# Changing the priority of the pole parameters, the patience for host stages and the order of the turned matmuls in a fused S4D and MLP kernel

## The chip, the core and the metric

The kernel runs on one NeuronCore of a Trainium2 chip. The metric is the device time of one launch in microseconds (us). The engines are TensorE (PE, the matmuls; its weight loads are listed as PEld), VectorE (DVE), ScalarE (ACT), GpSimd (POOL) and SyncE (SP, which here only issues DMAs). Each engine takes its instructions in program order and waits for others by semaphores. All matmuls write to PSUM, which has eight banks here called `cv` (four, as two pairs), `m0` to `m3`.

## The reference

```python
x  = A_u                                   # 1 x 2048 x 576
xn = layernorm(x)
# S4D: a long convolution along the 2048 positions, per channel d
A = -exp(log_A_real) + 1j * A_imag;  C = (C_real + 1j * C_imag) * dt      # 576 x 128, dt = exp(log_dt)
K[d, l] = 2 * Re(sum_n C[d, n] * exp(A[d, n] * dt[d] * l))
s = causal_convolution(xn, K) + xn * D_skip     # by an FFT of length 4096
# channel MLP on the same xn, with a second layernorm
h = gelu(layernorm(xn) @ w1 + b1)          # 2048 x 4608
g = silu(h @ w2 + b2)                      # 2048 x 576
out = x + s * g
```

Everything is float32. The kernel multiplies with the type fp32r and splits each operand of the MLP in a high and a low part, so that every product becomes three matmuls (high times high, high times low, low times high).

## The kernel before, in words

**The MLP carries the time axis.** The 4608 hidden units are cut into 12 groups of 384 (`NG = 12`, `G = 3` blocks of 128). The 2048 tokens are cut into two halves, and each half into two blocks of 512 tokens (`tb`). One group of one token block is a slot; there are 48 slots, in the order of `SETS`. A slot has 11 positions. The first three are layer 1, one block of 128 hidden units each: 14 matmuls of 512 columns (L546) into one bank, then gelu and a copy on ACT (L578, L581: `h`, `hh`) and a subtraction on DVE (L584: `hl`). The other eight are layer 2, in the order of the list `PLAN`, each entry a key and the hidden blocks it takes. The output's 576 columns are cut in 448 plain and 128 turned ones. A plain key 0 to 3 is a block of 128 tokens: stationary `hh` or `hl`, moving `w2s` with 448 columns (L638), into a bank that DVE then adds to `acc` (L643). The key `"T"` is the turned part: stationary `w2s`, moving `hh` or `hl` with 512 tokens (L630), accumulated in a bank of its own over many slots. Two banks, `m0` and `m1`, serve layer 1 and the plain keys by turns. Four slots (`TURNED`) use another form with 288 columns (L608, added by L615).

**Weights.** Each weight set (a group's `w1` and `w2`) comes through the tile `raw` by DMAs on SP (L473 to L478) and is split by ACT (L530) and DVE (L527) while the previous matmuls run. A set in `JOINED` has its `w2` split in three rows of 576 columns; any other is split apart, in 448, 384 and 896 columns, with the turned part as the second. `NEXT` says how many further raw loads each split issues: 1, 2, 2 for a joined `w2`, and 1, 0, 4 for one apart.

**The S4D part rides on the MLP.** Its matmuls are put between the positions of the slots. First come the parameters: `params()` builds from the four tables of poles and coefficients a polar form (magnitude, frequency and phase per pole), in the line `pl`: log_A_real is turned (L800) and goes through exp (L802), then C_real and C_imag are turned (L800), squared, and so on to an arctangent and sines (ACT) with reciprocals (DVE), then A_imag is turned. The four tables are fetched on SP (L793) at planned times in the list `fetch`. The result is packed and stored (`par_s`). Then 36 table stages make sines and magnitudes, and 36 guests (`kgen`, L981, 64 small matmuls each) turn them into the convolution's kernel. Six chunks of 96 channels each go through the stages `k1`, `x1` (L1053), `s2` (L1092), `inv` (L1145) and `i1` (L1177); these are the hosts. `i1` is followed by the stores of `s_s` (L1188). At the end, `combine_load`, `gated` (L711) and `summed` (L716) put together the output of the first half of the tokens, and `last_s` (L732), `finish` (L751 to L770) that of the second half.

**A planner sets the order.** The kernel is unrolled, and the order of all instructions on each engine is made by the class `Order`: it keeps an estimated clock for each engine, and lines of steps, each with an estimated length, a due time and the marks it needs. `advance` takes the step that can start first; of several that can start at the same time, the one whose line stands first in `od.lines`. In the early slots `row_lines` (L1333 on) rearranges that list. The line `nl` holds the layer norms of the blocks 4 to 15 of the tokens (L383 to L405); before the change it stands right ahead of `pl`. The order that comes out is fixed; if an engine is later in truth than in the plan, what stands behind waits.

**Where hosts and guests go.** `pe_turns` is called after every position, and on the positions given in `all_lines` it may put a host or a guest on PE. A paced host (`k1`, `x1`, `s2`) must come at least half of `(END - now) / left` after the one before it, `left` being the paced hosts still to come. A guest that is ready when a host is placed goes ahead of it in the same place (`ride`). Once the hosts have begun, a guest that finds no host goes alone when it has been ready for `ALONE` us (the last guest is exempt).

Of the kernel before, what the change touches and what calls it, by code (L numbers as in the profile page):

```python
# [23 lines left out]
NCH = D // CH  # L24
# [11 lines left out]
G = 3  # L36
# [7 lines left out]
def dve(n):  # L44
    return 0.075 + 0.00104 * n
# [163 lines left out]
def step(eng, dur, fn, need=(), mark=None, cv=0, at=0.0, late=0.0, tbl=None, by=1e9):  # L209
    return dict(eng=eng, dur=dur, fn=fn, need=tuple(need), mark=mark, cv=cv, at=at, late=late, tbl=tbl, by=by)  # L210
# [3 lines left out]
def mixer_kernel(ctx, tc, u, log_a_real, a_imag, c_real, c_imag, log_dt, d_skip, w1, b1, w2, b2,  # L214
# [238 lines left out]
    SEQ = [(n, g, tb) for n, (g, tbs) in enumerate(SETS) for tb in tbs]  # L453
    FIRST, GATE = (0, 3, 2 * NG, 2 * NG + 1), (2 * NG - 4, 2 * NG - 1)
    TURNED = (2 * NG - 4, 2 * NG - 1, 4 * NG - 2, 4 * NG - 1)
    JOINED = {SEQ[slot][0] for slot in TURNED} | set(range(6))
    DT = D - DA
    for n, (g, _) in enumerate(SETS):
        PARTS += [(n, g, 1, i) for i in range(KB + 1)] + [(n, g, 2, i) for i in range(G)]
# [37 lines left out]
    def split_raw(low_on=nc.vector):  # L497
# [14 lines left out]
        else:  # L512
            joined, m = half in JOINED, P
            if i == 0:
# [178 lines left out]
    def combine_load(b, n, c0, c1, part=None):  # L693
        m = c1 - c0
        if part is None:
            XS[b] = [sb.tile([P, D], F32, name="row", bufs=NROW)[:, :n * m].rearrange("p (i d) -> p i d", i=n) for _ in range(3)]
        elif part == 0:
            kt = [sb.tile([P, 12, 64], F32, name="kt", bufs=2).rearrange("p a b -> p (a b)") for _ in range(2)]
            xc = sb.tile([P, 2, 32, 24], F32, name="xc", bufs=NXC).rearrange("p a b c -> p (a b c)")
            XS[b] = [t[:, :n * m].rearrange("p (i d) -> p i d", i=n) for t in (kt[0], xc, kt[1])]  # L700
        x, s, g = XS[b]
        if part != 1:
            nc.gpsimd.dma_start(x, u_s[:, b:b + n, c0:c1])
            nc.gpsimd.dma_start(g, g_s[b:b + n, :, c0:c1].rearrange("i p d -> p i d"))
        if part != 0:
            nc.gpsimd.dma_start(s, s_s[:, b:b + n, c0:c1])
# [71 lines left out]
    def params():  # L778
# [10 lines left out]
        T = [p[:, :D] for p in PRM] + [ys_tile().rearrange("p i a b c -> p (i a b c)")[:, :D]]  # L789

        def load(k):
            for q in range(4):
                nc.sync.dma_start(PRM[k][32 * q:32 * q + 32, :D].rearrange("p (b j) -> p b j", j=32), dram(  # L793
                    src[k], 32 * q, [[N, 32], [32 * N, D // 32], [1, 32]]))
        fetch = [step(None, 6.0, lambda k=k: load(k), at=t, mark=("praw", k)) for k, t in ((0, 44.0), (2, 56.0), (3, 60.0), (1, 66.0))]
        add(None, 12.0, lambda: nc.sync.dma_start(dt, dram(log_dt, 0, [[0, P], [1, D]])), at=24.0)
        add("ACT", act(D), lambda: nc.scalar.activation(dt, dt, AF.Exp), tbl="exp", late=0.0)
        V, A = nc.vector, nc.scalar
# [16 lines left out]
        t = T[2]  # L815
# [394 lines left out]
    NPOS = G + 8  # L1210
    NSLOT = 4 * NG
    od = Order(tc, nc)
    od.pinned = True
    el, wl2, wl, nl2, pl, pl2, pl3, pl4, pl5, nl, ml, ml2, xl, wx, c3, c2, c1, kl, tl, sl, vl, gl, fl, f2l = [od.line() for _ in range(24)]
# [78 lines left out]
    MA, MT = 0.2034, 0.2303  # L1293
    CONV = {2 * NG - 6: 0, 2 * NG - 2: 1, 4 * NG - 4: 0, 4 * NG - 3: 1}
    both, allof = (0, 1), (0, 1, 2)
    PLAN = [("T", both), (0, both), ("T", (2,)), (0, (2,)), (1, allof), (2, allof), (3, (0,)), (3, (1, 2))]
    ENDS = {True: {2: 0, 3: 1, 5: 2, 7: 3}, False: {3: 0, 4: 1, 5: 2, 7: 3}}

    def lens(slot):
# [32 lines left out]
    def row_lines():  # L1332

        Y = [A2F[:, k:k + TB] for k in (2 * D, PT0 + 4 * D, 0, D, PT0 + 4 * D + TB, PT0 + 4 * D + 2 * TB)]
        X, T = [Y[k] for k in (0, 1, 2, 0, 3)], Y[4:]

        def store(t):
            nc.gpsimd.dma_start(dram(y4_s, t * P * D, [[D, 64], [64 * D, 2], [1, D]]), YT[4 + t])

        def load(i):  # L1340
            for q in range(4 if i < KB else 2):
                y = X[i][32 * q:32 * q + 32]
                if i < KB:
                    nc.gpsimd.dma_start(y.rearrange("p (b d) -> p b d", b=4), dram(
                        y4_s, i * P * D + P * q, [[D, 32], [32 * D, 4], [1, P]]))
                else:
                    nc.gpsimd.dma_start(y.rearrange("p (b j) -> p b j", j=32), dram(
                        y4_s, KB * P + 32 * q, [[D, 32], [32 * D, NT], [1, 32]]))

        def blocks(i):  # L1350
            x, y = T[i % 2], X[i]
            if i < KB:
                nc.vector.transpose(x.rearrange("p (k b t) -> p k b t", k=4, b=4),
                                    y.rearrange("p (b k j) -> p k b j", k=4, b=4))
            else:
                nc.vector.transpose(x[:64], y[:64])

        def places(i):
            y = T[i % 2]
            c = slice(i * P, (i + 1) * P)  # L1360
            if i < KB:
                return y.rearrange("p (k t) -> p k t", k=4), XH[:, :, 1, c], XL[:, :, 1, c]
            return y[:64], XR[:64, 1], XR[64:, 1]

        def high(i):
            y, h, _ = places(i)
            nc.scalar.activation(h, y, AF.Copy)

        def low(i):
            y, h, lo = places(i)  # L1370
            nc.vector.tensor_sub(lo, y, h.bitcast(F32))
        issue = od.line()
        for i in range(KB + 1):
            out = od.line()["steps"]
            if i < KB:
                out.append(step("POOL", 0.7, lambda i=i: store(i), need=[("yn", 4 + i)], mark=("yo", i)))
            out.append(step(None, 6.0, lambda: None, need=[("yo", min(i, 3))], mark=("ys", i)))
            issue["steps"].append(step("POOL", 2.4 if i < KB else 1.2, lambda i=i: load(i), mark=("yi", i),
                                       need=[("ys", i)] + ([("yt", 0)] if i == 3 else [])))
            od.line()["steps"].append(step(None, 5.0 if i < KB else 7.0, lambda: None, need=[("yi", i)], mark=("yl", i)))  # L1380
            a, b, c = od.line(), od.line(), od.line()
            a["steps"].append(step("DVE", dve(TB), lambda i=i: blocks(i), mark=("yt", i),
                                   need=[("yl", i)] + ([("y2", i - 2)] if i > 1 else [])))
            b["steps"].append(step("ACT", act(TB), lambda i=i: high(i), mark=("yh", i), need=[("yt", i)]))
            c["steps"].append(step("DVE", dve(TB), lambda i=i: low(i), need=[("yh", i)], mark=("y2", i) if i < KB else ("x", 1)))
        k = [i for i, x in enumerate(od.lines) if x is pl][0]
        od.lines = od.lines[-26:] + od.lines[:k] + [nl] + [x for x in od.lines[k:-26] if x is not nl]

    YB = []

# [102 lines left out]
    for k in range(4):  # L1493
        gl["steps"].append(step("POOL", 5.0, lambda k=k: part.update({k: load_g2(k)}), mark=("g2", k),
                                need=[("g2c", k - 1)] if k else []))
# [24 lines left out]
    def end_line():  # L1520
        for c, c0, c1, sets in ((NCH - 3, 0, CE, [(b, 1) for b in range(8)]), (NCH - 2, CE, CL, [(0, 4), (4, 4)])):
            for b, n in sets:
                a = (b, n, c0, c1)
                ml["steps"].append(step(None, 8.0 if b else 12.0, lambda a=a: combine_load(*a), need=[("st", c), ("u", NT - 1)]))
                ml["steps"].append(step("DVE", 2 * dve(n * (c1 - c0)), lambda a=a: (gated(*a), summed(*a))))
                ml["steps"].append(step(None, 4.0, lambda: None))
        a = (0, 8, CL, D)
        ml["steps"].append(step(None, 1.0, lambda: combine_load(*a, 0), need=[("k1", NCH - 1, 1), ("x1", NCH - 1)]))
        ml["steps"].append(step(None, 11.0, lambda: combine_load(*a, 1), need=[("st", NCH - 1)]))
        ml["steps"].append(step("DVE", dve(8 * CH) + 0.1, lambda: gated(*a)))  # L1530
        ml["steps"].append(step("DVE", dve(8 * CH) + 0.1, lambda: summed(*a)))


    pace = dict(left=NCH * (2 + 2 + 4), last=0.0, started=False)
    END = 930.0
    ALONE = 5.0

    def pe_turns(limit=1, any_time=False, all_lines=True):
        for x in (nl, pl, ml) + ((c3, c1, kl) if all_lines else ()):
# [29 lines left out]
    later(mid - 4, G - 1, lambda: x_free(0))  # L1569
    later(mid - 1, G - 1, lambda: x_free(1))  # L1570
    later(NSLOT - 10, 4, end_line)
    sl["steps"].append(step(None, 11.0, last_s, need=[("st", NCH - 1)], mark="s8"))
    for k in range(8):
        c3["steps"].append(step(None, 5.0 if k == 0 else 2.0, lambda k=k: last_x(k), need=[("i1", NCH - 1), ("u", NT - 1)], mark=("x8", k)))

# [49 lines left out]
    for slot in range(NSLOT):  # L1625
# [4 lines left out]
        for pos in range(NPOS):  # L1630
            if pos < G:
                need = wmark(n, 1) + [("x", tb)]
# [16 lines left out]
                for k, (a, b, c) in enumerate(cell, pos + 1 - len(cell)):  # L1649
                    by = hidden_by(pos, k)  # L1650
                    if slot == NSLOT - 1 and k:
                        a = seeded(a, tb, k)
# [6 lines left out]
            else:  # L1659
# [6 lines left out]
                need = [wmark(n, 2)[i] for i in w2_parts(n, j, hid)] + [("h", slot, i) for i in hid]  # L1666
# [19 lines left out]
                if last or halves:  # L1686
                    add = cell[0]
                    dh, k = (terms[0][1], 1) if halves else (0, 2)
# [9 lines left out]
                    if final:  # L1698
                        b = 8 + 4 * tb + j
                        x, y = (el, el2) if slot < NSLOT - 1 else (od.line(),) * 2  # L1700
# [13 lines left out]
            for f in LATER.get((slot, pos), ()):  # L1714
                f()
            od.advance(od.t["PE"])
            pe_turns(all_lines=pos in (0, 1, G + 1, G + 3, G + 5, NPOS - 1))
    od.force(lambda: not od.urgent and not any(x["steps"] for x in od.lines))


# [52 lines left out]
```

## Time and profile before

| what | value |
|---|---|
| median of 3 runs | 1068.91 us (1068.3 to 1071.31) |
| the profiled execution | 1070.33 us |
| its span, first to last instruction | 1068.2 us |
| PE busy | 1057.6 us, 99% |
| DVE busy | 936.7 us, 88% |
| ACT busy | 677.4 us, 63% |
| POOL busy | 212.2 us, 20% |
| granted PE clock | 0.999 |

The profile is of one execution. Its time differs from the span by what lies before the first and after the last instruction. A row of the order of time gives the start, the length, the engine and line, what is written and read, the shapes, how many instructions are merged in the row, and in brackets the engine's idle time before it with what ended it. Matmuls are pipelined: the length of one is longer than the step from its start to the next one's start, and it is the step that adds up. A row of a stretch gives its bounds and length, then for PE, PEld, DVE, ACT and POOL the busy time and the count, then the PE clock, the DMA share and GB/s.

### The profile page before, as it was taken

How to read it: one execution, taken by the hardware profiler on the slowest of the kernel's cores; microseconds unless marked ns; L12 is line 12 of the kernel's file. 1: busy time of each engine (PE TensorE's matmuls, PEld its weight loads, DVE VectorE, ACT ScalarE, POOL GpSimd, SP SyncE). 2: the span in 40 equal slices, each digit the busy share in tenths (PEclk: the TensorE clock that was granted, in tenths of full speed). 3: DMA queues.
4: the chain of work that ended last, by engine and by line, in shares of the span. 5: the costliest groups of instructions: out<-in, count | busy, mean ns of one | idle time of the engine just before them, and what ended most of it. 6: DMA issues, size and time to landing. Idle time of an engine off the chain costs nothing. (4 is left out here: it accounts for less than half of the span.)

```text
span 1068.2 us, 23535 instructions
## 1 busy us (share of the span) xinstructions
PE 1057.6 (99%) x9515; PEld 874.5 (82%) x9515; DVE 936.7 (88%) x1550; ACT 677.4 (63%) x1056; POOL 212.2 (20%) x294
## 2 busy tenths in 40 slices
PE   9999999999999999999999999999999999999997
PEld 7887888888878887888878888788877888778886
DVE  7688768889999899999999999899899999957656
ACT  6567639877655767657667675666685675625344
POOL 5668743201000002000120000200002022322020
PEclk9999999999999999999999999999999999999999
DMA  7885446664223143454521315222421446465145
GB/s 230 238 259 171 121 144 224 214 163 142 62 69 91 43 100 99 120 134 116 124 83 48 110 39 121 74 75 64 96 86 45 132 118 150 125 188 162 24 126 170
DMA packets 149213, 130.93 MB, mean 123 GB/s; under 512 B 99020, under 2 KB 121072, under 8 KB 148080
## 3 DMA queue, kind: packets, MB, share of 16 engines
q1 hardware_dynamic: 132592, 79.76, 28.2%
q0 software_dynamic: 15760, 48.70, 14.9%
q8 instruction: 75, 1.23, 0.5%
q10 hardware_dynamic: 752, 0.97, 0.3%
q14 instruction: 34, 0.28, 0.1%
HBM read 98.90 MB, written 35.19 MB: 126 GB/s over the span
## 5 line engine op out<-in xcount | busy, mean ns | idle before, releaser
L638 PE MATMUL m<-w2s,hh 128*128 128x448 f32 x1056 | 301.9, 367 | 0.4 <-DVE acc L643 0.2
L638 PEld LDWEIGHTS m<-w2s,hh 128*128 128x128 f32 x1056 | 196.1, 188 | 28.9 <-issue 7.0
L578 ACT ACTIVATE h<-m,b1t 128x512 f32<-128x512 f32 x144 | 99.2, 689 | 188.2 <-PE m L546 183.6
L638 PE MATMUL m<-w2s,hl 128*128 128x448 f32 x528 | 191.5, 363 | 0.0
L546 PE MATMUL m<-XH,w1h 128*128 128x512 f32 x564 | 155.5, 398 | 0.0
L546 PE MATMUL m<-XL,w1h 128*128 128x512 f32 x564 | 151.6, 391 | 0.0
L546 PE MATMUL m<-XH,w1l 128*128 128x512 f32 x564 | 151.0, 390 | 0.0
L584 DVE TENSOR_TENSOR hl<-h,hh 128x512 fp32r<-128x512 f32 x144 | 99.1, 689 | 53.7 <-ACT hh L581 53.3
L546 PEld LDWEIGHTS m<-XH,w1h 128*128 128x128 f32 x564 | 103.4, 188 | 30.9 <-issue 9.1
L546 PEld LDWEIGHTS m<-XL,w1h 128*128 128x128 f32 x564 | 105.9, 188 | 23.0
L546 PEld LDWEIGHTS m<-XH,w1l 128*128 128x128 f32 x564 | 105.9, 188 | 22.4
L881 POOL DMA_DIRECT2D par<-par_s x36 | 27.4, 762 | 484.2 <-DVE mg L924 423.7
L643 DVE TENSOR_TENSOR acc<-m,acc 128x448 f32<-128x448 f32 x160 | 98.4, 615 | 19.0 <-PE m L638 17.7
L638 PEld LDWEIGHTS m<-w2s,hl 128*128 128x128 f32 x528 | 99.1, 188 | 7.4
L630 PE MATMUL m<-hh,w2s 128*128 128x512 f32 x264 | 98.9, 402 | 0.0
L581 ACT ACTIVATE hh<-h 128x512 fp32r<-128x512 f32 x144 | 90.6, 630 | 3.3
L530 ACT ACTIVATE w2s<-raw 128x576 fp32r<-128x576 f32 (+3 forms) x75 | 46.4, 675 | 48.6 <-PE m L638 47.0
L924 DVE TENSOR_TENSOR mg<-par 128x1024 f32<-128x1024 f32 x72 | 67.9, 952 | 0.7
L630 PEld LDWEIGHTS m<-hh,w2s 128*128 128x128 f32 x264 | 49.6, 188 | 17.5 <-issue 5.1
L527 DVE TENSOR_TENSOR w1l<-raw,w1h 128x384 fp32r<-128x384 f32 x98 | 49.8, 558 | 13.8 <-ACT w1h L530 13.7
L546 PE MATMUL m<-XR,w1r 128*128 128x512 f32 x141 | 54.9, 389 | 0.0
L546 PE MATMUL m<-XR,w1s 128*128 128x512 f32 x141 | 54.9, 389 | 0.0
(227 smaller groups left out, 1866.3 us busy)
## 6 DMA issues: line engine op xcount, KB each, us to landing
raw<-in_B_w_dram SPq DMA_DIRECT2D x75, 288.0 KB, 3.5
raw<-in_B_w_dram SPq DMA_DIRECT2D x100, 192.0 KB, 3.4
par_s<-A POOLq DMA_DIRECT2D x8, 1080.0 KB, 5.6
par<-par_s POOLq DMA_DIRECT2D x36, 240.0 KB, 3.4
f2t<-f2q SPq DMA_DIRECT2D x24, 256.0 KB, 3.8
raw<-in_B_w_dram SPq DMA_DIRECT2D x50, 96.0 KB, 3.9
u_s<-in_A_u_dram POOLq DMA_DIRECT2D x16, 288.0 KB, 4.1
xc<-xn_s SPq DMA_DIRECT2D x48, 96.0 KB, 4.1
```

What stands on the lines that cost most here:

```text
L527: low_on.tensor_sub(lo, r[:m], h[:m].bitcast(F32))
L530: nc.scalar.activation(h, r, AF.Copy)
L546: nc.tensor.matmul(q, a, b, start=j == 0, stop=j == len(ops) - 1)
L578: nc.scalar.activation(t, q, AF.Gelu_apprx_tanh, bias=b1t[:, g * G + i:g * G + i + 1], scale=1.0)
L581: LAST[0] = nc.scalar.activation(hh[:, i], t, AF.Copy)
L584: nc.vector.tensor_sub(hl[:, i], t, hh[:, i].bitcast(F32))
L630: nc.tensor.matmul(q, a[:, i], b[:, i], start=first and i == 0 and k == 0, stop=slot in CONV and i == G - 1 and k == 2, skip_group_check=True)
L638: nc.tensor.matmul(q[:, :DA], a[:, i, key * P:key * P + P], b[:, i], start=i == 0 and k == 0, stop=i == G - 1 and k == 2)
L643: nc.vector.tensor_add(o, Q2.pop(key)[:, :DA], bias2[:, :DA] if first else o)
L881: nc.gpsimd.dma_start(PAR[b].rearrange("p (g i) k -> p g (i k)", g=4), dram(par_s, (b // 6 * CH + b % 6 * 4) * NPAR, [[D * NPAR, P], [24 * ...
L924: nc.vector.tensor_mul(T["m"][:, :, 64 * k:64 * k + 8 * n].rearrange("p c (i j) -> p c i j", i=n), bc(PAR[b][:, :, e8:e8 + n], 3, 8), bc(P ...
```

## The change

Seven edits are made together.

- `JOINED` keeps only the weight sets 0 and 1 of the first six; the sets 2 to 5 are now split apart.
- The list `fetch` asks for C_real first, at 44, then log_A_real at 50, C_imag at 56 and A_imag at 62. Before, it was log_A_real at 44, C_real at 56, C_imag at 60 and A_imag at 66.
- `PLAN` begins with the two first hidden blocks of the plain key 0, and the nine turned matmuls follow as one stretch.
- `row_lines` puts `pl` ahead of `nl`.
- The planned time from the last chunk's stores to the landing of its loads is 16 us instead of 11 in `end_line` and 14 instead of 11 in `last_s`.
- `END` is 960 instead of 930, and `ALONE` is 9 instead of 5.
- Hosts and guests may be placed after position G + 2 instead of G + 1.

```diff
-    JOINED = {SEQ[slot][0] for slot in TURNED} | set(range(6))
+    JOINED = {SEQ[slot][0] for slot in TURNED} | {0, 1}
...
-        fetch = [step(None, 6.0, lambda k=k: load(k), at=t, mark=("praw", k)) for k, t in ((0, 44.0), (2, 56.0), (3, 60.0), (1, 66.0))]
+        fetch = [step(None, 6.0, lambda k=k: load(k), at=t, mark=("praw", k)) for k, t in ((2, 44.0), (0, 50.0), (3, 56.0), (1, 62.0))]
...
-    PLAN = [("T", both), (0, both), ("T", (2,)), (0, (2,)), (1, allof), (2, allof), (3, (0,)), (3, (1, 2))]
+    PLAN = [(0, both), ("T", both), ("T", (2,)), (0, (2,)), (1, allof), (2, allof), (3, (0,)), (3, (1, 2))]
...
-        od.lines = od.lines[-26:] + od.lines[:k] + [nl] + [x for x in od.lines[k:-26] if x is not nl]
+        first = [pl, nl]
+        od.lines = od.lines[-26:] + od.lines[:k] + first + [x for x in od.lines[k:-26] if all(x is not y for y in first)]
...
-        ml["steps"].append(step(None, 11.0, lambda: combine_load(*a, 1), need=[("st", NCH - 1)]))
+        ml["steps"].append(step(None, 16.0, lambda: combine_load(*a, 1), need=[("st", NCH - 1)]))
...
-    END = 930.0
-    ALONE = 5.0
+    END = 960.0
+    ALONE = 9.0
...
-    sl["steps"].append(step(None, 11.0, last_s, need=[("st", NCH - 1)], mark="s8"))
+    sl["steps"].append(step(None, 14.0, last_s, need=[("st", NCH - 1)], mark="s8"))
...
-            pe_turns(all_lines=pos in (0, 1, G + 1, G + 3, G + 5, NPOS - 1))
+            pe_turns(all_lines=pos in (0, 1, G + 2, G + 3, G + 5, NPOS - 1))
```

## The prediction

> **What bounds the kernel now.** I read the page first, then the waits of TensorE (PE), then PE's instructions in order of time around each wait and around the guests.
>
> ```profile
> span 1068.2 us, 23535 instructions
> PE 1057.6 (99%) x9515; PEld 874.5 (82%) x9515; DVE 936.7 (88%) x1550; ACT 677.4 (63%) x1056; POOL 212.2 (20%) x294
> ...
> PE m L630 <- DVE hl L584: 1.3, 2, 1.0
> ```
>
> PE is at work for 99% of the span; its named waits are of this size, two of together 1.3 us here and one of 1.34 us that is shown below. So the end is set by the number of matmuls, by the gaps that a change of matmul kind leaves between them, and by these few waits. An edit off PE gains nothing unless it removes such a gap or wait, and it costs something only when it makes one. The sum below is made against the profiled execution, 1070.33 us (its span and 2.1 us around it); the median of the runs is 1068.91 us, 1.4 us less, and I carry the differences over to that.
>
> **The order of the terms in layer 2.** The new plan puts six plain matmuls (`(0, both)`) ahead of the turned ones, so that a slot has one turned stretch instead of two.
>
> ```profile
> 158.70 0.39 PE L630 MATMUL m<-hh,w2s 128*128 128x512 f32 x1
> 158.93 0.57 PE L638 MATMUL m<-w2s,hh 128*128 128x448 f32 x2
> ...
> 159.94 0.36 PE L638 MATMUL m<-w2s,hl 128*128 128x448 f32 x1
> 160.14 0.40 PE L630 MATMUL m<-hh,w2s 128*128 128x512 f32 x1
> 160.37 0.39 PE L630 MATMUL m<-hl,w2s 128*128 128x512 f32 x1
> ```
>
> Start to start, turned to plain takes 0.23 us, plain to turned 0.20, turned to turned 0.23: the first matmul's length decides, and the change of kind adds nothing. The 44 slots with this plan gain 0 from it; a rounding step of 0.01 on each of the two changes that go would be 0.9 us, and I put the bounds at 0 and -0.9. The first L2 step now needs all of `w2s`' plain part rather than its turned part. These splits run in the L1 stretch, under 9.5 us of matmuls; the last of them is the third DVE instruction of the row below, over at 209.29, six us ahead of the slot's L2 at 215.43.
>
> ```profile
> 207.20 2.09 DVE L527 TENSOR_TENSOR w2s<-raw,w2s 128x448 fp32r<-128x448 f32 x3
> ...
> 215.43 0.39 PE L630 MATMUL m<-hh,w2s 128*128 128x512 f32 x1
> ```
>
> The four weight sets taken out of `JOINED` (numbers 2 to 5, slots 2 to 9) get the same three splits by ACT and DVE, cut 448, 384 and 896 wide instead of 3 x 576: the same 1728 columns, so 0. Without that cover the price would be the last split itself, about 1 us a set. Their raw loads on SP move: one after the first split, four after the third, instead of 1, 2 and 2. That matters for the queue below. The place for hosts that moves from after step G+1 to after G+2 only shifts a host by three matmuls: 0.
>
> **Patience.** A table guest that has been ready for 5 us goes alone; the new limit is 9 us.
>
> ```profile
> 394.81 0.36 PE L638 MATMUL m<-w2s,hl 128*128 128x448 f32 x1
> 395.10 1.10 PE L981 MATMUL cv<-v,U 128*32 128x64 f32 x64
> 396.13 0.68 PE L638 MATMUL m<-w2s,hh 128*128 128x448 f32 x2
> 396.65 0.36 PE L638 MATMUL m<-w2s,hl 128*128 128x448 f32 x1
> 396.85 0.56 PE L638 MATMUL m<-w2s,hh 128*128 128x448 f32 x2
> 397.25 0.36 PE L638 MATMUL m<-w2s,hl 128*128 128x448 f32 x1
> ...
> 399.94 1.62 PE L1177 MATMUL cv<-A,g1t 64*32 64x384 f32 x32
> ...
> 905.12 1.10 PE L981 MATMUL cv<-v,U 128*32 128x64 f32 x64
> ...
> 908.15 1.25 PE L1177 MATMUL cv<-A,g1t 64*32 64x384 f32 x24
> ```
>
> A guest's entry takes 395.10 - 394.81 = 0.29 us where matmuls follow each other after 0.20, and the two matmuls behind it take 396.65 - 396.13 = 0.52 instead of 0.40. These 0.21 us are shared when it rides in front of a host, so 0.2 is what a ride saves. Six guests, the first at 395.10 and the last at 905.12, went alone less than 5 us ahead of a host that did not depend on them. With 4 us more patience each should ride: -1.2 us. Bounds: 11 guests went alone after the hosts began, so at most -2.3; or five that ride now miss their host, +1.0.
>
> **Slack at the end.** DVE waited in `gated` for a load of `s`, and PE waited behind it for an accumulation.
>
> ```profile
> 1040.37 0.30 PE L608 MATMUL m<-w2s,hl 128*128 128x288 f32 x1
> 1042.01 0.54 PE L608 MATMUL m<-w2s,hh 128*128 128x288 f32 x2 [1.34 <-DVE acc L615]
> ...
> 1040.63 0.96 DVE L711 TENSOR_TENSOR xc<-xc,kt 128x768 f32<-128x768 f32 x1 [2.36 <-DMA xc<-s_s]
> ```
>
> The step from 1040.37 to 1042.01 is 1.64 us instead of 0.13, and the pair behind it 0.54 instead of 0.43: 1.6 us. Planning that load at 16 us instead of 11 places `gated` 5 us later, after the landing that ended the 2.36 us wait. I take -1.6; bounds 0 (another wait takes its place) and -1.6. The 14 us for the other load of `s` moves DVE work that has its data in time already: 0.
>
> **The pacing end of 960.** The spacing of the paced stages is half of (end - now)/left, so 30 us more lengthens a lower limit. In the last chunk the stages wait for data, not for this limit: 14.2 us from its last `inv` to its `i1` (rows under the rivals). I take 0 for it, and the bad end is a rival of its own.
>
> **The polar form first.** `pl` now wins DVE ahead of `nl` whenever both are ready. What decides is whether its data is there, because DVE takes instructions in order.
>
> ```profile
> 53.13 2.52 SPq L475 DMA_DIRECT2D raw<-in_B_w_dram  x3
> 55.71 2.98 SPq L358 DMA_DIRECT2D w<-in_A_u_dram  x6
> ...
> 63.76 5.11 SPq L793 DMA_DIRECT2D pr<-in_A_C_real_dram  x4
> 68.91 2.40 SPq L793 DMA_DIRECT2D mg<-in_A_C_imag_dram  x4
> ...
> 62.00:70.00 8.00, 8.00 (x41) 7.34 (x40) 7.50 (x16) 4.53 (x7) 2.63 (x2) 1.00 1.04 342
> ...
> 62.66 1.28 ACT L802 ACT_TABLE_LOAD   x1
> 63.95 0.69 ACT L802 ACTIVATE A<-A 128x576 f32<-128x576 f32 x1
> ...
> 66.63 0.62 DVE L643 TENSOR_TENSOR acc<-m,acc 128x448 f32<-128x448 f32 x1
> ...
> 71.54 0.78 DVE L800 STREAM_TRANSPOSE xc<-pr 128x576 f32<-128x576 f32 x1 [1.69 <-DMA pr<-in_A_C_real_dram]
> ...
> 69.92 1.07 PE L546 MATMUL m<-XH,w1h 128*128 128x512 f32 x4
> 90.98 0.39 PE L546 MATMUL m<-XH,w1h 128*128 128x512 f32 x1
> ...
> 166.91 1.07 PE L546 MATMUL m<-XH,w1h 128*128 128x512 f32 x4
> 185.78 1.07 PE L546 MATMUL m<-XH,w1h 128*128 128x512 f32 x4
> ```
>
> C_real was asked for at 56, issued at 63.76 behind the eight loads of `u`, and held DVE for 1.69 us at 71.54; the DMA share of 1.04 from 62 to 70 says that the engines were full. The DVE was dense after that, and the lateness came out on PE: the slot from 69.92 to 90.98 took 21.06 us, where a clean one takes 185.78 - 166.91 = 18.87, so 2.2 us were lost, 1.8 of them by the two waits for `hl`. Now C_real is asked for at 44, where log_A_real stood, and log_A_real at 50, ahead of the raw loads that SP issues from 53.13, so both come early. But C_imag is asked for at 56, C_real's old place behind the loads of `u`. I estimate its landing at 70.3: SP gets to those loads about 2 us sooner, since no second split stands before them, but two more w1 loads come ahead of it. Bounds 67.5 (ahead of all w1 loads) and 73 (behind a full queue).
>
> In `pl` the transposes follow the exp of log_A, which ends at 64.64. With the norms behind it, C_real's transpose comes at once, and C_imag's right after the accumulation at 66.63, at 67.2. DVE then waits 3.1 us there, where it waited 1.69 later. Queued behind it is the next accumulation (0.61), whose bank the layer 1 at 69.92 writes again: 70.3 + 0.8 + 0.6 = 71.7, so PE stands 1.8 us there, and the rest of the lateness comes out at `hl`. A wait of 1.69 became 1.8, so 3.1 becomes about 3.3: +1.5 us. Bounds: -1.8 (C_imag is there) and +4.2 (it lands at 73). What `pl` pushes back, the norms of blocks 8 to 15, feeds POOL's `xn_s` stores and the tables, which no matmul needs before the guests at about 200 us.
>
> ACT left one function table for the next in 63.95 - 62.66 = 1.29 us, the load alone. The Trainium skill (ScalarE: Activation LUTs, What ACT_TABLE_LOAD costs) gives 2.66 us for a switch, 1.38 of them a drain. By it the polar form's exp and back would hold ACT 2.8 us longer before the gelu of the next slot, and the sum would be up to 2.8 us higher; this trace shows no such drain, and I follow the row.
>
> **The sum.** 0 (order) - 1.2 (rides) - 1.6 (end) + 1.5 (C_imag) = -1.3: 1069.0 us for the profiled execution, 1067.6 us for the median. Its own range is 1065 to 1071.
>
> **The rivals.**
>
> 1. C_imag is there in time, or its transpose comes later. Then the 1.8 us go instead: -1.2 - 1.6 - 1.8 = -4.6, 1064.3 us. For it: the fetches stand 4 us earlier, and C_real at 44 takes 295 KB out of the crowd. Against: SP's order and the full engines.
>
> 2. The last `i1` comes too late: the side that is slower.
>
> ```profile
> 1009.89 1.56 PE L1145 MATMUL cv<-ys,g2t 32*64 32x192 f32 x64
> ...
> 1024.08 1.62 PE L1177 MATMUL cv<-A,g1t 64*32 64x384 f32 x32
> ...
> L732 SPq DMA_DIRECT2D v<-s_s x2: 431/856/1281, 1037.3 to 1038.6; - x2
> ...
> DMA to landing us min/median/max: 1.8/1.9/4.2
> ...
> 1045.10:1064.80 19.70, 17.58 (x107) 15.88 (x106) 14.63 (x23) 11.23 (x22) 0.42 (x1) 1.00 0.56 150
> ```
>
> The last `s` was issued at 1038.6 and was there 1.9 to 4.2 us later, about 1041.6; DVE's last stretch began at 1045.1, 3.5 us after, and had 19.70 - 15.88 = 3.8 us free. So `i1` may slip by 7.3 us, to 1031.4; from there each us is a us at the end. One guest that misses its host in the last chunk holds up the next table and `k1`; a slip as long as from `inv` to `i1`, 14.2 us, gives 6.9 - 1.2 - 1.6 + 1.5 = +5.6, 1074.5 us. For it: the later pacing end, and the patience, which delays the guests that the last `k1` needs. Against: the earlier polar form starts the tables sooner, and the limit hardly binds at the end.
>
> 3. The order by hand is only shuffled: rides won are lost elsewhere, and one wait replaces another. 0: 1068.9 us.
>
> **How the numbers follow.** About 0.3%, 3.2 us, is what a measurement of this kernel can tell from no change. The forecast has 0.40 (0.06 faster, 0.30 same, 0.04 slower), rival 1 0.28 (0.25 faster, 0.03 same), rival 2 0.18 (0.02 same, 0.16 slower), rival 3 0.14 (0.02, 0.10, 0.02). Together 0.33 faster, 0.45 same, 0.22 slower. The range runs from a little under rival 1, 1063.3, to the middle of rival 2's slips, 1073.3.
>
> **What would show it.** Right: the transpose of `mg` waits for C_imag near 67 us and PE stands near 70; of the 36 guests, the 14 that go alone fall to about eight; no PE wait near 1040; PE's step at a change of kind is unchanged. Wrong: no DVE wait on C_imag, the last `i1` after 1031, or a new PE wait over 1 us anywhere in the middle.

## The result, and the profile after

The changed kernel takes 1081.5 us (1080.44 to 1081.86), against 1068.91 us before: a ratio of 1.0108, with an interval of 1.0096 to 1.012 (the two medians alone would give 1.0118). The change is slower by about 1.1%, and the time is outside the range of the prediction. The profiled execution took 1081.86 us against 1070.33.

The head of the page, and then the waits of PE, of the changed kernel (engine and what waited, what it waited for: us in total, how often, the longest):

```profile
span 1080.1 us, 23532 instructions
PE 1059.9 (98%) x9515; PEld 875.9 (81%) x9515; DVE 935.0 (87%) x1550; ACT 690.7 (64%) x1068; POOL 208.3 (19%) x294
```

```profile
PE cv L1177 <- DVE A L1161: 7.1, 1, 7.1
PE cv L1092 <- DMA f2t<-f2q: 3.0, 1, 3.0
```

Before, no wait of PE was longer than 1.34 us. Now there is one of 7.1 us ahead of the last chunk's `i1`, and one of 3.0 us ahead of an `s2`. The first of them, in the order of time of the changed kernel (PE, then SP, ACT and DVE):

```profile
1031.15 0.39 PE L546 MATMUL m<-XR,w1s 128*128 128x512 f32 x1
1038.63 2.94 PE L1177 MATMUL cv<-A,g1t 64*32 64x384 f32 x32 [7.09 <-DVE A L1161]
1041.50 2.03 PE L546 MATMUL m<-XH,w1h 128*128 128x512 f32 x4
1043.36 1.07 PE L546 MATMUL m<-XL,w1h 128*128 128x512 f32 x4
...
1019.36 11.04 SPq L663 DMA_DIRECT2D acc<-bias  x16
1031.73 0.33 SPq L665 DMA_DIRECT2D bias<-in_B_b_dram  x1
1032.12 0.42 SPq L473 DMA_DIRECT2D raw<-in_B_w_dram  x1
...
1035.80 0.68 ACT L530 ACTIVATE w2s<-raw 128x576 fp32r<-128x576 f32 x1 [9.35 <-DMA raw<-in_B_w_dram]
...
1036.52 0.76 DVE L527 TENSOR_TENSOR w2s<-raw,w2s 128x576 fp32r<-128x576 f32 x1 [8.43 <-ACT w2s L530]
1037.19 1.30 DVE L1161 STREAM_TRANSPOSE A<-A 128x512 f32<-128x512 f32 x2
```

Read from the bottom: `i1` waits for two transposes on DVE; they stand behind the low part of the third `w2` row (L527), that behind ACT's high part (L530), and that behind the raw load of 1032.12. The load stands on SP behind `place_rest` (L663, 16 small transfers that put the turned part of a token block's sum in its place: 11.04 us of issues) and behind the bias load (L665), which waits until these transfers have read the tile that it overwrites. The planner charges 1.0 us of SP for all of `place_rest`.

The same place before, SP and PE:

```profile
1012.84 1.72 SPq L473 DMA_DIRECT2D raw<-in_B_w_dram  x3
1016.89 10.61 SPq L663 DMA_DIRECT2D acc<-bias  x16
...
1023.76 0.39 PE L546 MATMUL m<-XR,w1s 128*128 128x512 f32 x1
1026.69 1.09 PE L546 MATMUL m<-XL,w1h 128*128 128x512 f32 x4
```

There all three raw loads were issued ahead of `place_rest`. From the last layer-1 matmul ahead of `i1` to the fifth behind it took 1026.69 - 1023.76 = 2.93 us; now it takes 1043.36 - 1031.15 = 12.21: 9.3 us more, 7.1 of them the wait and the rest slower matmuls behind it. Why the order on SP turned round is seen in the order of time of DVE (the kernel before), and then of DVE and PE (the changed one):

```profile
1013.66 0.54 DVE L527 TENSOR_TENSOR w1s<-raw,w1r 64x384 fp32r<-64x384 f32 x1
1014.97 0.75 DVE L651 TENSOR_SCALAR acc<-m,tv 128x512 f32<-128x512 f32 x1 [0.77 <-PE m L630]
```

```profile
1017.49 0.75 DVE L651 TENSOR_SCALAR acc<-m,tv 128x512 f32<-128x512 f32 x1
1019.69 0.54 DVE L527 TENSOR_TENSOR w1s<-raw,w1r 64x384 fp32r<-64x384 f32 x1
...
1017.38 1.56 PE L1145 MATMUL cv<-ys,g2t 32*64 32x192 f32 x64
```

The last raw load is issued after the last split of `w1` (L527, `w1s`), `place_rest` after the end of the turned stretch (L651). The host `inv` (L1145) stood ahead of layer 2 of this slot, at 1009.89; now it stands behind the turned stretch, at 1017.38. So the turned stretch ends before the splits are through (L651 at 1017.49, the last `w1s` split at 1019.69), and `place_rest` gets to SP ahead of the third raw load.

The second wait, changed kernel (PE and SP), and then the kernel before:

```profile
508.29 2.76 PE L1092 MATMUL cv<-A,f2t 64*32 64x192 f32 x64 [2.97 <-DMA f2t<-f2q]
...
489.69 11.85 SPq L663 DMA_DIRECT2D acc<-bias  x16
503.39 0.42 SPq L1031 DMA_DIRECT2D f2t<-f2q  x1
```

```profile
501.65 0.42 SPq L1031 DMA_DIRECT2D f2t<-f2q  x1
...
506.31 1.60 PE L1092 MATMUL cv<-A,f2t 64*32 64x192 f32 x64
```

Here `f2t` stood behind `place_rest` before too, but the load came at 501.65 and the matmul at 506.31, 4.7 us later. Now the load is 1.7 us later, and PE would have been ready 1 us sooner, at 508.29 - 2.97 = 505.3. The wait is 3.0 us and the 64 matmuls take 2.76 instead of 1.60: 4.1 us in all.

The sum over PE: I take for each host and guest the time from the matmul ahead of it to the third behind it, less those matmuls' own steps. That was 137.5 us in all and is 149.0 now; by this measure the two waits with the slow matmuls make 13.1 of it (9.0 and 4.2), so the rest of the hosts and guests got cheaper by 1.6. The waits of PE between other matmuls were 5.3 us and are 5.9: the 1.6 near 1040 are gone, and 2.2 of new small ones came. 13.1 - 1.6 + 0.6 = 12.1, and the span grew by 11.9. So the whole loss lies on PE, and the two waits with what follows them are a little more than all of it.

The early part, changed kernel (DVE, ACT, PE):

```profile
69.59 0.78 DVE L800 STREAM_TRANSPOSE A<-mg 128x576 f32<-128x576 f32 x1 [1.59 <-DMA mg<-in_A_C_imag_dram]
...
53.94 0.53 ACT L530 ACTIVATE w2s<-raw 128x384 fp32r<-128x384 f32 x1 [2.11 <-DMA raw<-in_B_w_dram]
...
57.89 1.19 PE L546 MATMUL m<-XH,w1h 128*128 128x512 f32 x4 [0.28 <-ACT h L578]
71.58 1.16 PE L546 MATMUL m<-XH,w1h 128*128 128x512 f32 x4 [0.93 <-DVE acc L643]
151.24 1.20 PE L546 MATMUL m<-XH,w1h 128*128 128x512 f32 x4 [0.85 <-DVE acc L643]
```

### The profile page after: what moved, and what is told of

Read it like the earlier page. It is cut to its first block, busy times and chain, and to the rows that moved or that the text cites. A ratio compares the mean times of both kernels' runs of the same rounds, so it can differ in the third digit from the quotient of the medians.

```text
span 1080.1 us, 23532 instructions
## 1 busy us (share of the span) xinstructions
PE 1059.9 (98%) x9515; PEld 875.9 (81%) x9515; DVE 935.0 (87%) x1550; ACT 690.7 (64%) x1068; POOL 208.3 (19%) x294
## 4 chain that ended last, share of the span: by engine, by line
PE 82%; DVE 5%; DMA 4%; POOL 3%; SPq 2%; ACT 2%; issue 2%; ACTq 0%; DVEq 0%; POOLq 0%
PE m L546 36%; PE m L638 25%; PE m L630 7%; PE cv L981 3%; PE cv L1092 3%; PE m L608 3%; SPq L663 2%; PE cv L1053 2%; PE cv L1145 1%; DMA raw<-in_B_w_dram 1%; PE cv L1177 1%; DMA f2q<-in_f_dram 1%; POOL A L1344 1%; PE m L561 1%; POOL v L414 1%
## 5 line engine op out<-in xcount | busy, mean ns | idle before, releaser
L630 PE MATMUL m<-hh,w2s 128*128 128x512 f32 x264 | 89.1, 391 | 0.0
L530 ACT ACTIVATE w2s<-raw 128x448 fp32r<-128x448 f32 (+3 forms) x75 | 46.9, 677 | 53.7 <-PE m L638 39.8
L905 ACT ACTIVATE w<-w 128x1024 int32<-128x1024 f32 x36 | 38.1, 1058 | 46.4 <-DVE w L902 46.3
L527 DVE TENSOR_TENSOR w2s<-raw,w2s 128x448 fp32r<-128x448 f32 (+3 forms) x75 | 54.0, 747 | 13.1 <-ACT w2s L530 13.0
```

The lines of the kernel that those rows point to most:

```text
L527: low_on.tensor_sub(lo, r[:m], h[:m].bitcast(F32))
L530: nc.scalar.activation(h, r, AF.Copy)
L630: nc.tensor.matmul(q, a[:, i], b[:, i], start=first and i == 0 and k == 0, stop=slot in CONV and i == G - 1 and k == 2, skip_group_check=True)
L905: nc.scalar.activation(T["w"][:, 0].bitcast(I32), T["w"][:, 1], AF.Copy)
```

## The experiments

**Theory Q** (SP's queue): `place_rest` holds SP for 11 us where 1 was planned, and what stands behind it comes late. **Rival R**: the longer patience and the later END make the last guests and hosts late by themselves. "POOL (1, 3)" below is this edit, with the calls of `place_rest` counted from 0 (in runs 5 to 7 written as `tb == 1`, which is the same two calls):

```diff
     def place_rest(tb):
+        queue = nc.gpsimd if placed[0] in (1, 3) else nc.sync
+        placed[0] += 1
...
-                nc.sync.dma_start(o[32 * v:32 * v + 32, :, 32 * c:32 * c + 32], x[32 * c:32 * c + 32, :, v])
+                queue.dma_start(o[32 * v:32 * v + 32, :, 32 * c:32 * c + 32], x[32 * c:32 * c + 32, :, v])
         if tb == 1:
-            nc.sync.dma_start(bias2[:, :DA], dram(b2, 0, [[0, P], [1, DA]]))
+            queue.dma_start(bias2[:, :DA], dram(b2, 0, [[0, P], [1, DA]]))
```

**1. All four on POOL, the bias load left on SP.**

```diff
-                nc.sync.dma_start(o[32 * v:32 * v + 32, :, 32 * c:32 * c + 32], x[32 * c:32 * c + 32, :, v])
+                nc.gpsimd.dma_start(o[32 * v:32 * v + 32, :, 32 * c:32 * c + 32], x[32 * c:32 * c + 32, :, v])
```

> The changed kernel whole, with one edit: the 16 small transfers of place_rest are issued by POOL and no longer by SP. Theory Q (SP's queue): place_rest holds SP for 11 us, and a w2 row of the last chunk's hosts (near 1032) and the f2t load (near 503) stand behind it; with it off SP both matmul waits (7.1 and 3.0 us) and the slow matmuls after them (1.8 and 1.2 us) go: 1081.5 - 9.0 - 4.2 = 1068.3 us, granted clock back near 1.00. Rival R (patience): the guests of the last chunk start later because hosts wait longer for them, and place_rest merely stands nearby: the wait ahead of i1 stays above 5 us and the time at 1080 us or above.

Measured 1081.72 us, 1.0115 (1.0098 to 1.0132). Both signs named for R came: the time is above 1080, and the wait ahead of `i1` is still above 5 us. The trace shows why that does not decide for R (waits of PE; order of time of POOL and SP):

```profile
PE cv L1177 <- DVE A L1161: 5.2, 1, 5.2
PE m L630 <- DVE hl L584: 2.2, 2, 2.0
```

```profile
1019.57 8.69 POOL L663 DMA_DIRECT2D acc<-bias  x16 [13.97 <-DVE bias L655]
...
1029.69 0.33 SPq L665 DMA_DIRECT2D bias<-in_B_b_dram  x1
1030.13 0.36 SPq L473 DMA_DIRECT2D raw<-in_B_w_dram  x1
```

The wait for `f2t` is gone, but the raw load still came only at 1030.13: the bias load ahead of it on SP waits for the POOL transfers to have read their tile. And the first `place_rest`, now on POOL, pushed the `par` loads back to 411.91 (the first of them stood at 405.39 in the changed kernel), for 2 us of a new PE wait at 423.86. The experiment had not taken the queue away.

**2. The place of the hosts taken back** in the changed kernel.

```diff
-            pe_turns(all_lines=pos in (0, 1, G + 2, G + 3, G + 5, NPOS - 1))
+            pe_turns(all_lines=pos in (0, 1, G + 1, G + 3, G + 5, NPOS - 1))
```

> The changed kernel with the one edit of pe_turns taken back: hosts that run on all lines stand again at position G+1 and not G+2 of a slot. Theory Q: the last chunk's host comes early enough that its w2 rows are issued ahead of the last place_rest, and f2t ahead of the first one; both waits go: 1068 us, within 1.5. Rival R (patience of 9 and the later END alone make the last guests late): 1079 us or above, with a wait of 5 us or more ahead of the last i1.

1073.32 us, 1.0037 (1.0022 to 1.0051). Both waits are gone with patience and END still in, which is against R; the time is 5 us above what Q gave. 2.2 of them are small waits of PE between other matmuls (8.1 us in all, 5.9 in the changed kernel); the median lies 1.8 us above the profiled execution (1071.5), so part of it is in executions without a trace; the rest isn't accounted for. In this run `inv` stands inside the turned stretch, at 1015.60, the stretch ends after the last split, and all three raw loads (1016.42) go ahead of `place_rest` (1020.01).

**3. PLAN and the place of the hosts alone**, on the kernel before.

> The kernel before with only the order of the turned matmuls (PLAN) and the place of the hosts (G+1 to G+2) changed. Theory Q: the third w2 row of the last chunk goes behind the last place_rest on SP, and the matmul i1 waits about 7 us for it, plus about 1.8 us of slower matmuls: 1078 us, within 2. Rival R: no patience was added, so no late guest: 1069 us.

1085.25 us, 1.0146 (1.0131 to 1.0161): above what Q gave, and slower than the whole change, without any patience. As the whole cause R falls. The longest wait of PE, and another one in PE's order of time:

```profile
PE m L546 <- ACT h L578: 5.5, 1, 5.5
```

```profile
1004.65 2.27 PE L1092 MATMUL cv<-A,f2t 64*32 64x192 f32 x64 [2.51 <-DMA f2t<-f2q]
```

This time the late `w2` row holds a gelu that stands behind its split on ACT, and `f2t` stands behind the third `place_rest`. Not all of the loss is on PE: its last matmul starts at 1071.13, 8.7 us later than before, but the span (1083.8) is 15.6 us longer. The last `i1` came only at 1050.43; run 10 shows what that does.

**4. All four on POOL in the kernel before**, with the diff of run 1.

> The kernel before with one edit: the 16 small transfers of place_rest on POOL. Theory Q: nothing in it waits for what stands behind place_rest on SP, so 1068.9 us, within 1. Rival R says the same; a gain above 1 us here would say that SP's queue cost the kernel before something too, and a loss that POOL is a worse place for these transfers.

1068.28 us, 0.9994 (0.9985 to 1.0003): no difference, as said.

**5. The changed kernel with POOL (1, 3).**

> The changed kernel with the second and the fourth place_rest (near 490 and 1019 us) and the bias load behind the fourth issued by POOL; the first and third stay on SP. Moving all four had left the bias load on SP, where it waited for the transfers with the w2 row behind it, and had put a par load on POOL back near 411. Theory Q (what stands behind place_rest on SP is the whole loss): no wait ahead of i1 and s2, clock back near 1.00, no wait near 421: 1081.5 - 9.0 - 4.2 = 1068.3 us, and up to 1071 where the early part costs what the run with the hosts put back showed. Rival R (late guests): a wait of 5 us or more ahead of i1, 1078 us or above.

1069.14 us, ratio 1.0 (0.9987 to 1.0013): 12.4 us of the change's 12.6 us loss go by moving the issue of 34 transfers. The order of the instructions on PE, DVE and ACT is the same in both traces, so that only the queues differ. The order of time of run 5 (SP, POOL, PE):

```profile
1013.89 3.06 SPq L473 DMA_DIRECT2D raw<-in_B_w_dram  x3
...
1015.99 8.71 POOL L664 DMA_DIRECT2D acc<-bias  x16 [29.34 <-DVE bias L655]
...
1027.79 1.62 PE L1178 MATMUL cv<-A,g1t 64*32 64x384 f32 x32
```

Q holds. All the rest of the change together is worth nothing measurable, which leaves the question what its parts cost and bring.

**6. As 5, with the first six sets joined again.**

```diff
-    JOINED = {SEQ[slot][0] for slot in TURNED} | {0, 1}
+    JOINED = {SEQ[slot][0] for slot in TURNED} | set(range(6))
```

> As the run with the two place_rest calls on POOL, and the JOINED set back to the first six halves (one ACT and one DVE split per w2 row there, as before). Theory J (splitting in three costs early time: the second split waits for the third row at 53.9, and the first gelu's h comes 1.1 us later): the PE waits near 57 and 150 us go, 1 to 2 us below the run beside it. Rival (nothing: my figure in the prediction): within 0.5 us of it.

1070.99 us, 1.0025 (1.0014 to 1.0036): 1.9 us slower than run 5, not faster. The PE wait near 57 goes, but those near 70 and 150 grow by 0.8 us together. So splitting apart is a gain in this plan. The waits of PE name only 0.2 us of it, and the profiled executions differ by 0.9 (spans 1068.1 and 1067.2): what it comes from isn't shown.

**7. `pl` first and the new loads alone**, on the kernel before, with POOL for the second and fourth `place_rest`.

```diff
-        for k, t in ((0, 44.0), (2, 56.0), (3, 60.0), (1, 66.0))]
+        for k, t in ((2, 44.0), (0, 50.0), (3, 56.0), (1, 62.0))]
...
-        od.lines = od.lines[-26:] + od.lines[:k] + [nl] + [x for x in od.lines[k:-26] if x is not nl]
+        od.lines = od.lines[-26:] + od.lines[:k] + [pl, nl] + [x for x in od.lines[k:-26] if x is not pl and x is not nl]
```

> The kernel before with only pl put ahead of nl and the four praw loads in the new order and times (and the two place_rest calls and the bias load on POOL, which keeps SP's queue out of it). Prediction's term: +1.5 us, so 1070.3 us, with a PE wait near 70 us for C_imag of about 1 us. Rival (C_imag in time): 1068.9 us or a little less, no wait near 70.

1076.17 us, 1.0075 (1.006 to 1.009). Not a clean run: the moved bias load stands 5 us on POOL with a `par` load behind it (order of time of POOL, DVE and PE).

```profile
510.06 0.57 POOL L666 DMA_DIRECT2D bias<-in_B_b_dram  x1 [4.97 <-issue]
...
514.47 1.23 DVE L900 TENSOR_TENSOR w<-par,tv 128x1024 f32<-128x1024 f32 x1 [3.10 <-DMA par<-par_s]
...
517.08 0.56 PE L608 MATMUL m<-w2s,hl 128*128 128x288 f32 x1 [3.36 <-DVE hl L584]
```

**8. The slack of 16 alone**, on the kernel before (11.0 to 16.0 at `combine_load(*a, 1)`).

> The kernel before with only the slack of the last combine_load raised from 11 to 16 us. Prediction's term: the PE wait of 1.3 us near 1040 us goes and the end comes 1.6 us earlier: 1067.3 us. Rival (the DVE work that made it late is only put elsewhere): 1068.9 us, with a wait of about 1 us at another place after 1040.

1066.56 us, 0.9978 (0.9968 to 0.9987): 2.4 us faster, faster than both kernels, and no wait of PE near 1040 is left.

**9. As 7, with only the fourth on POOL.**

> The run of the front alone again (pl ahead of nl, the loads in the new order, on the kernel before), with only the fourth place_rest and its bias load on POOL: with the second one there too, a par load stood on POOL behind the bias load, and a matmul waited 3.4 us near 513. Prediction's term +1.5 us: 1070.4 us. By the PE waits near 70 (1.4 to 1.8 us) and 150 us (1.4 to 1.7), less the 1.6 us of waits near 80 that go: +1.5 to +2, so 1070.5 to 1071 us. Rival (the 7.2 us of the disturbed run belong to the front itself): 1074 us or above.

1073.0 us, 1.0039 (1.0024 to 1.0053): +3.9. PE's losses near 71 (1.9) and 150 us (1.5 and 0.4) are 3.8 us against the 2.2 that the prediction found near 80 before: +1.6, the size of my term. The rest is in waits of 0.2 to 0.6 us near 247, 497 and 515, where the later plan has moved.

**10. As 3, with POOL (2, 3).**

> The run of the order alone again (PLAN and the place of the hosts, on the kernel before), with the third and fourth place_rest and the bias load on POOL. Theory Q: all of its 16.3 us are what stood behind place_rest on SP, the order of the terms itself costs nothing, as the prediction had it: 1069 us, within 1.5. Rival (the order of the terms or the later host costs by itself): 1072 us or above, with waits left that no queue explains.

1072.39 us, 1.0032 (1.0019 to 1.0045): 12.9 of the 16.3 us go, and by the time it is the rival's 1072. What is left isn't PE. Its order of time (PE, DVE), and then PE's end before:

```profile
1037.00 1.58 PE L1181 MATMUL cv<-A,g1t 64*32 64x384 f32 x32
1057.70 0.29 PE L608 MATMUL m<-w2s,hl 128*128 128x288 f32 x1
...
1065.22 0.46 DVE L771 TENSOR_TENSOR A<-A,v 128x288 f32<-128x288 f32 x1
```

```profile
1062.39 0.29 PE L608 MATMUL m<-w2s,hl 128*128 128x288 f32 x1
```

PE is done 4.7 us earlier than before, but its last `i1` stands at 1037.00, 12.9 us later, and the DVE work behind it ends the kernel 2.3 us later (spans 1070.5 and 1068.2). This is rival 2's mechanism, seen alone. By it the end would be 1037.0 - 1031.4 = 5.6 us later; it is 2.3, so I estimate the point from which it decides at 1037.0 - 2.3 = 1034.7.

**11. As 5, with ALONE 5 and END 930.**

> As the run with two place_rest calls on POOL (1069.1 us), with the patience taken back: ALONE 5 and END 930. Prediction's term: 0.2 us for each guest that loses its ride, seven of them, so 1.2 to 1.6 us more: 1070.5 us. Rival (patience bought nothing): 1069.1 us, within 0.4.

1075.9 us, 1.0061 (1.0044 to 1.0077): 6.8 us more than run 5. Of the 36 guests 15 go alone instead of 7, and hosts and guests take 2.8 us more (138.7 and 135.9), 1.2 of it a wait of one `s2`. Another 3.2 us are PE waits for adds and low parts near 470 to 498. They follow a wait of DVE: 3.83 us at 464.94 for rows of `y_s`. SP issued a group of twelve of these loads from 456.16 on; in run 5 it did so from 442.61. So only the 2.8 us are what hosts and guests lose; the 3.2 follow loads that come later on SP in this plan.

**12. As 5, with the loads due at 44, 48, 52 and 56.**

> As the run with two place_rest calls on POOL (1069.1 us), with the four praw loads due at 44, 48, 52 and 56 us and no longer at 44, 50, 56 and 62. If the wait near 70 us is for the landing of C_imag alone, it goes (1.4 us) and the time is 1067.7 us; if the earlier loads push others back, the wait only moves: 1069.1 us or more, with a wait between 50 and 70 us.

1069.32 us, 0.9999 (0.999 to 1.0009). PE's loss near 70 falls from 1.4 to 0.9 us, that near 57 rises from 0.6 to 1.5 and that near 150 from 1.0 to 1.5: the wait only moves.

**13. `pl` first with the old loads**, on the kernel before, with the fourth on POOL (the second part of the diff of run 7).

> The kernel before with only pl put ahead of nl (the four praw loads as before), and the fourth place_rest with its bias load on POOL. Theory: the place of pl is the cost of the front: the par products of the norms (L899, L902) come onto DVE near 150 us and wait there for their par load, with the adds and low parts that PE waits for behind them (1.5 to 1.9 us of PE waits near 150 us), and the transpose of C_imag near 67 waits for the old, later load, so a PE wait near 70 us of 2 us or more: 1073 us or above, as with the new loads or worse. Rival (the new loads are the cost): 1069.5 us or less, with no PE wait near 150 us.

1080.78 us, 1.011 (1.0091 to 1.0129). The longest wait of PE, and DVE's order of time:

```profile
PE m L638 <- DVE acc L643: 4.0, 1, 4.0
```

```profile
70.36 0.78 DVE L804 STREAM_TRANSPOSE xc<-pr 128x576 f32<-128x576 f32 x1 [4.73 <-DMA pr<-in_A_C_real_dram]
```

With the old loads DVE waits 4.73 us for C_real near 70, and PE 4.0 us behind it; with the slow matmuls that follow, PE loses 6.8 us there. But 6.1 us more are lost near 475, where DVE had waited for rows of `y_s`, 3.02 and 1.78 us, and PE then 3.17 us behind it:

```profile
462.55 10.63 SPq L1402 DMA_DIRECT2D row<-y_s  x16
```

That is again a long group of issues on SP, as `place_rest` is, and not the front itself. So `pl` first is the costly half, and the new loads take back most of it (1.9 us near 71 in run 9, against 6.8), but not all of the 12 us are its price. The loss near 150 us that I expected here does not show.

**14. PLAN and the slack of 16**, on the kernel before, with the fourth on POOL.

> The kernel before with only PLAN changed and the slack of the last combine_load at 16, and the fourth place_rest with its bias load on POOL. By the prediction the order of the terms is worth nothing, so the time is that of the slack alone: 1066.6 us, within 1. Rival (the order with the first matmuls on their own frees PE, as the run of the order showed PE ending 4.7 us earlier): 1064.5 us or less. Rival (it costs): 1068 us or more.

1067.11 us, 0.9988 (0.9979 to 0.9998), 0.55 us from the slack alone (run 8). Against the kernel before that was measured beside each, run 14 gained 1.1 us and run 8 2.4, and the intervals of the two ratios overlap: the order of the terms, with the hosts left in their place, is worth nothing that these runs can tell, though a cost of about 1 us isn't excluded. The order of time of SP and POOL:

```profile
1012.71 1.72 SPq L473 DMA_DIRECT2D raw<-in_B_w_dram  x3
...
1017.00 8.69 POOL L667 DMA_DIRECT2D acc<-bias  x16 [34.66 <-DVE bias L655]
```

`inv` stands ahead of layer 2 here, at 1009.76, as in the kernel before, and all three raw loads go ahead of `place_rest`.

**15. As 14, with the last slack at 14 and END at 960.**

> As the run beside it (PLAN, slack 16, fourth place_rest on POOL), with the last slack at 14 and END at 960 as in the change. By the prediction END and the last slack are worth nothing: the time of the run beside it, within 0.7 us. Rival: the last i1 moves later and the end with it, 1 us more or above.

1068.15 us, 0.9998 (0.9988 to 1.0007), 1 us more. PE's order of time:

```profile
507.20 1.60 PE L1096 MATMUL cv<-A,f2t 64*32 64x192 f32 x64 [2.36 <-DMA f2t<-f2q]
```

`f2t` stands behind the second `place_rest` on SP, as in the changed kernel, though the hosts are in their old place.

**16. As 15, with POOL (1, 3).**

> As the run with PLAN, both slacks and END (1068.15 us), with the second place_rest and its bias load on POOL too. Theory Q: the wait of 2.4 us for f2t near 507 is all that END cost; it goes: 1065.7 us, within 0.7, and that is the fastest of all. Rival (END costs by the later i1): 1068 us, or only the wait moves.

1066.26 us, 0.9974 (0.9965 to 0.9984). The wait is gone and so is the microsecond; with run 8 this is the fastest of these versions, 2.2 to 2.4 us ahead of the kernel before. The two can't be told apart.

## Why the prediction was wrong

The step that failed is in "The order of the terms in layer 2": "The place for hosts that moves from after step G+1 to after G+2 only shifts a host by three matmuls: 0." On PE that holds. But the host that moved let the turned stretch end ahead of the weight splits, and with it `place_rest` went past the raw load on SP. I had looked at SP only near 60 us. Taking this edit back removes both waits (run 2), it and PLAN alone bring waits of the same kind (run 3), and taking the second and fourth `place_rest` off SP removes the loss whole (run 5). In place of the 0 stand the 9.0 us at the raw load and a part of the 4.2 at `f2t`.

Where `inv` stands tells the runs apart. Ahead of the turned stretch (the kernel before, run 14) or inside it, a host pushes back the end of the stretch, and `place_rest` with it; behind it (the changed kernel) or later (run 3, 1023.61) it pushes back nothing, and `place_rest` comes ahead of the third raw load. With the new PLAN the place after G+1 lies inside the stretch (run 2 at 1015.60; run 15 at 1012.26, between turned matmuls at 1011.94 and 1013.75), and the place after G+2 behind it. PLAN alone did not turn the order: in run 14 the three raw loads go at 1012.71 and `place_rest` at 1017.00. It was on POOL there, but in runs 4 and 5 moving it to POOL left the order on PE, DVE and ACT as it was. The place after G+2 without PLAN was not run. The second wait needs less: `f2t` stood behind `place_rest` before as well, 4.7 us in time, and run 15 has a wait of 2.36 us for it with the hosts in their old place.

- **Order of the terms: 0, right** as far as PLAN goes and the runs can tell (run 14). In run 10 PE even ended 4.7 us earlier, more than the bound of 0.9 allows. The profile names 3.0 us less of waits of PE there (1.9 in all, 4.9 before), and some of those waits, near 80 us, are missing in run 8 too, which has the order of before. So it isn't the change of kind that the bound was for.
- **JOINED: 0, wrong by a little.** The second split waited 2.11 us for the third raw row at 53.94 in the changed kernel, and PE lost 0.4 us near 57; against that, run 6 shows that joining them again costs 1.9 us.
- **Rides: -1.2, right in the count** (14 alone became 7, I said about 8) and nearly in size, -1.6 in the changed kernel. The whole edit was worth 6.8 us where run 11 took it out, but only 2.8 of that is hosts and guests; the 3.2 that followed SP's later loads were in no term of mine.
- **Slack: -1.6, right.** The wait near 1040 is gone, and alone the edit brought 2.4 us (run 8). In run 4, with the order of before on PE, DVE and ACT, that wait was only 0.30 us (at 1041.66), so its size differs from one execution to the next, and where all of the 2.4 come from isn't shown.
- **END: 0.** Right once the queue is out of it (run 16, 1066.26 us, is no slower than run 14, 1067.11); with the second `place_rest` on SP it came with a loss of 1 us (run 15).
- **C_imag: +1.5, right in place and nearly in size.** DVE waited 1.59 us at 69.59 where I had 3.1 near 67; PE lost 1.1 us near 70, and 1.4 near 150, which I hadn't named. Alone on the kernel before the front cost 3.9 us (run 9), 1.6 of it by these waits. That this meets my +1.5 is partly luck: half of the 3.8 us lies near 150, where I had nothing, and the 2.2 us that I took off as lost near 80 belong mostly to the one execution that was profiled: in runs 4 and 8, with the same order on PE, the profile names no wait there.
- **The table switch.** In the changed kernel the load for the same exp starts at 63.29 and the exp at 64.59, 1.30 us, the load alone as before. The 2.8 us more that the prediction names as the other possibility did not come.
- **Rival 2** had the place right (the last `i1`, which came at 1038.63, after its point of 1031.4) and the sign, but not the cause. A weight row was late, and not a guest that missed its host. And its price was too low, since PE stood behind the waiting `i1`: every microsecond of the 7.1 counted, and not only those after a slack.

Of what I named as a sign of being wrong, two came: the last `i1` after 1031, and a new PE wait over 1 us in the middle.

## What to carry to other kernels

When a planner's order is moved, each queue has to be read for what goes past what, at every place where a long group of issues stands, not only where the edit is aimed: here 16 small transfers that the plan took for 1 us held SP for 11, and the old order missed the trouble by a few microseconds. Price such a group at its measured length, or give it a queue on which nothing urgent stands behind it, and move with it whatever waits for it. A time that doesn't change when a cause is taken away (run 1) doesn't clear the cause until the trace shows that it is really gone.

## What the runs showed of the hardware

PE's matmuls slow down after waits of 2.5 us and more. Stretches of the changed kernel and of run 5 (bounds and length; busy us and count of PE, PEld, DVE, ACT, POOL; granted PE clock, DMA share, GB/s):

```profile
500.00:525.00 25.00, 22.03 (x239) 19.15 (x239) 18.73 (x39) 18.25 (x30) 1.08 (x2) 0.93 0.71 145
1025.00:1050.00 25.00, 17.91 (x108) 13.90 (x107) 8.26 (x15) 7.82 (x12) 4.72 (x9) 0.86 0.31 75
```

```profile
500.00:525.00 25.00, 24.65 (x255) 21.60 (x254) 22.05 (x46) 21.25 (x36) 2.76 (x5) 1.00 0.53 122
1025.00:1050.00 25.00, 25.00 (x166) 21.25 (x165) 14.78 (x25) 12.22 (x20) 7.41 (x12) 1.00 0.64 173
```

With waits of 2.97 and 7.09 us the granted clock over 25 us was 0.93 and 0.86, without them 1.00. Behind the short wait the 64 matmuls took 2.76 instead of 1.60 us, behind the long one `i1` took 2.94 instead of 1.62 and the next four matmuls 2.03, where such a row has 1.07 elsewhere. So a wait of 3 us cost 4.1, and one of 7.1 cost 9.3. The Trainium skill (TensorE: Matmul & The Clock Gate, HAM oscillation — how this bites in real kernels) warns of idle gaps over about 3.4 us; here a gap of 2.97 us was enough, so the measured one decides.

The other runs narrow it down. After 2.51 us in run 3 the 64 matmuls took 2.27 and the next four 2.06 instead of 1.07; after 2.36 us in run 15 they took 1.60, as without a wait. After 3.17 us in run 13 pairs of 448 columns took 0.95 us instead of 0.56, and it was 5.8 us before the steps were back to normal.

The 16 issues of the fourth `place_rest` took 11.0 us on SP (0.69 each) and 8.7 us on POOL (0.54 each).
